# Linear attention and a feed-forward pair on one core: where the loads of batch 1 are issued, and three smaller edits

## The chip, the cores and the metric

The kernel runs on one NeuronCore of a Trainium2 chip, as one program. The metric is the device time of one execution in microseconds (us). The core has a matrix engine (TensorE, here PE), a vector engine (VectorE, DVE), a scalar engine (ScalarE, ACT), a general engine (GpSimd, POOL or Pool) and an engine that issues DMAs (SyncE, SP). ACT and Pool issue DMAs too. Each engine runs its own instructions in order; 16 DMA engines move the data. SBUF is the memory on the core, PSUM the accumulators of PE.

## The reference

Inputs are q, k and v of shape (8, 8, 576, 64), that is batch, heads, sequence, head width, and two weight matrices of 512 x 2048 and 2048 x 512, all float32. The output is 4608 x 512 in float32.

```python
theta = np.pi / 2.0 * pos / S
cos_w, sin_w = np.cos(theta), np.sin(theta)      # along the sequence
def phi(x, c, s):
    r = np.maximum(x, 0.0)
    return np.concatenate([r * c, r * s], axis=-1)
q_p, k_p = phi(q, cos_w, sin_w), phi(k, cos_w, sin_w)
kv = np.einsum('bhsf,bhsd->bhfd', k_p, v)
z = np.sum(k_p, axis=2)
num = np.einsum('bhsf,bhfd->bhsd', q_p, kv)
den = np.einsum('bhsf,bhf->bhs', q_p, z)[..., None] + 1e-06
attn = num / den
x = attn.transpose(0, 2, 1, 3).reshape(B * S, H * D)
h = x @ w_in
g = h * (1.0 / (1.0 + np.exp(-1.702 * h)))
out = g @ w_out
```

## The kernel before

The attention of batch b gives columns of xT, a bf16 tensor of 128 partitions x 4 x 4608 tokens in SBUF. The feed-forward pair runs over nine blocks of 512 tokens. Block i takes 32 steps: 16 of mm1 (four matmuls of 128 x 512, then the activation by ACT) and 16 of mm2 (four matmuls each; every fourth step ends one chunk t of 128 tokens, which is copied to ysb and stored). The attention of batch b = i + 1 is cut into pieces, and a list `work[n]` puts each piece behind step n of block i. The schedule is written out by hand: each engine gets its instructions in the order of the program. Batch 0 runs ahead of the loop, and warm-up matmuls on zeros fill PE there (L75).

For each batch, q, k and v come as three main loads (`load_mains`, rows 0 to 511 of the sequence, 1 MB each, runs of 1 KB) and three tail loads (`load_tails`, rows 512 to 575, 128 KB each, runs of 256 bytes). SP issues both in batches 1 to 7; in batch 0 ACT issues the tails. q goes through max(x, 0) into qn (L217), is transposed by PE for batches 0 and 1 (L240) and by DMA later (L251), and is multiplied by cos and sin into qT (L244 or L256). v is multiplied by cos and sin into vt (L277), k goes through max into kr. `unit_kv` (L288) forms kv and z, `unit_den` the denominator (L309, L313) and its reciprocal (L318), `unit_spread` (L333) spreads that over partitions, `unit_num` (L351) forms the numerator, and L354 writes xT.

The weights are loaded by Pool in four quarters each. DMAs and copies of one element into `junk` are put in the queues as gates: SP's first one (L432) waits for the third quarter of w_in and stands ahead of the loads of batch 1; Pool's (L436) waits for batch 1's v and stands ahead of w_out; SP's second one (L439) waits for the third quarter of w_out and stands ahead of the loads of batch 2. Loads of batch 3 and later are issued at step 1 of the block two before.

In `unit_den` a matmul with three rows of constants (L309) puts 1e-6 into the accumulator, and the 32 matmuls of L313 add to it. The copies of mm2 go to ysb, which has three buffers, so the fourth chunk reuses the first's; in block 0 chunks 1 and 3 are copied by DVE (L401), all others by ACT (L403). SP issues all stores (L405). A chunk of 128 tokens is stored in one or two pieces; the last of all has two.

Of the kernel before, what the change touches and what calls it, by code (L numbers as in the profile page):

```python
# [12 lines left out]
F32 = mybir.dt.float32  # L13
# [8 lines left out]
ADD = mybir.AluOpType.add  # L22
# [6 lines left out]
def kernel(  # L29
# [9 lines left out]
    nc = tc.nc  # L39
    B, H, S, D = q.shape  # L40
    d_model = H * D
    d_ff = moe_w_in.shape[1]
    NP = H // 2
    FC = d_ff // 128
    TB = 512
    NBLK = B * S // TB
    HF = S // 2
    NSEG = 4
    SEG = S // NSEG
# [13 lines left out]
    def hps_tile():  # L63
        return ps.tile([128, TB], F32, name="hps", bufs=2)

    def yps_tile():
        return ps.tile([128, TB], F32, name="yps", bufs=2)

    def at_tile():
        return ps.tile([128, TB], F32, name="at", bufs=4)  # L70

    def warmup(n):
        for _ in range(n):
            wps = hps_tile()
            nc.tensor.matmul(wps, warm[:, 0:128], warm, start=True, stop=True)  # L75
# [8 lines left out]
    def load_tail(t, src, b, on):  # L84
        on.dma_start(
            out=t[0:64, 2048:2560].rearrange("p (h d) -> p h d", h=H),
            in_=src[b, :, 512:576, :].rearrange("h p d -> p h d"))
# [7 lines left out]
    def load_tails(b, on):  # L95
        for name, src in SRC:
            load_tail(state[b][name], src, b, on)
# [64 lines left out]
    ypool = ctx.enter_context(tc.tile_pool(name="ypool", bufs=3))  # L162
# [17 lines left out]
    ones = const.tile([3, 128], BF16)  # L180
    epsm = const.tile([3, SEG], BF16)
# [19 lines left out]
    w_in_sb = one.tile([128, NP, d_ff], BF16)  # L201
    w_out_sb = one.tile([128, FC, d_model], BF16)
# [16 lines left out]
    def prep_q(b, par, on=nc.vector):  # L219

        s = state[b]
        o = s["qn"].rearrange("p c (jo par hh) d -> p par c jo hh d", par=2, hh=2)[:, par]
        i = s["qf"][:, 0:2048].rearrange("p (jo par hh c d) -> p par c jo hh d", par=2, hh=2, c=4, d=D)[:, par]
        it = s["qf"][0:64, 2048:2560].rearrange("p (jo par hh d) -> p par jo hh d", par=2, hh=2, d=D)[:, par]
        for n in range(2):
            if par == 0:
                relu(on, o[:, 0:4, n], i[:, :, n])
            else:
                relu(on, o[:, 0:4, :, 1 - n], i[:, :, :, n])
                relu(on, o[0:64, 4, :, 1 - n], it[:, :, n])  # L230
        if par == 0:
            relu(on, o[0:64, 4], it)

    def transpose_pe(b, j, step):
        s = state[b]
        if step == 0:
            s["tp", j] = tp = at_tile().bitcast(BF16)
            for c in range(5):
                np_ = 128 if c < 4 else 64
                nc.tensor.transpose(tp[:, c * 128:c * 128 + np_],  # L240
                                    s["qn"][:np_, c, 2 * j:2 * j + 2, :].rearrange("p h d -> p (h d)"),
                                    ident[:np_, :np_])
            return
        nc.vector.tensor_tensor(s["qT"][:, j], s["tp", j][:, 0:S].unsqueeze(1).to_broadcast([128, 2, S]), trig, op=MUL)  # L244
# [13 lines left out]
    def prep_k(b, h0, h1, on=nc.vector):  # L258
        relu(on, kr[:, 0:4, h0 // 2:h1 // 2].rearrange("p c j (hh d) -> p (j hh) c d", hh=2),
             state[b]["kf"][:, 256 * h0:256 * h1].rearrange("p (h c d) -> p h c d", c=4, d=D))  # L260
# [44 lines left out]
    def unit_den(b):  # L305

        s = state[b]
        den_ps = at_tile()
        nc.tensor.matmul(den_ps[:, 0:SEG], ones[0:3, :], epsm[0:3, :], start=True, stop=False)  # L309
        for g in range(NSEG):  # L310
            for cs in range(2):
                for j in range(NP):
                    nc.tensor.matmul(den_ps[32 * j:32 * j + 32, 0:SEG], s["zs"][:, j, cs, ds(12 - 4 * g, 32)],  # L313
                                     s["qT"][:, j, cs, ds(g * SEG, SEG)],
                                     start=False, stop=(g == NSEG - 1 and cs == 1))
        inv, pa, pb, comb = [two.tile([128, SEG], dt, name=f"den{n}", bufs=1)
                             for n, dt in enumerate((F32, F32, F32, BF16))]
        nc.vector.reciprocal(inv, den_ps[:, 0:SEG])  # L318
        for o, m in ((pa, 0), (pb, 1)):
            nc.vector.tensor_tensor(o.bitcast(I32), inv.bitcast(I32), bits[:, m:m + 1].to_broadcast([128, SEG]), op=AND)  # L320
        nc.vector.tensor_tensor(comb, pa, pb, op=SUB)
        s["comb"] = comb
        s["invb"] = {}
# [33 lines left out]
    gT = {}  # L357
# [16 lines left out]
    def pieces(m):  # L374

        got, g = [], m * 128
        while g < m * 128 + 128:
            b, r = divmod(g, S)
            if r < 512:
                n = min(128 - r % 128, m * 128 + 128 - g)  # L380
                got.append((g - m * 128, n, b * S + 4 * (r % 128) + r // 128, 4))
            else:
                n = min(S - r, m * 128 + 128 - g)
                got.append((g - m * 128, n, b * S + r, 1))
            g += n
        return got
# [3 lines left out]
    def mm2(i, t, part):  # L390

        if part == 0:
            cur[t] = hps_tile() if i == 0 and t < 2 else yps_tile()
        yps = cur[t]
        for fc in range(part * 4, part * 4 + 4):
            nc.tensor.matmul(yps, gT[fc][:, ds(t * 128, 128)], w_out_sb[:, fc, :],  # L396
                             start=(fc == 0), stop=(fc == FC - 1))
        if part == 3:
            ysb = ypool.tile([128, d_model], F32, name="ysb")
            if i == 0 and t % 2:  # L400
                nc.vector.tensor_copy(ysb, yps)  # L401
            else:
                nc.scalar.copy(ysb, yps)  # L403
            for (p0, n, row, step) in pieces(i * 4 + t):
                nc.sync.dma_start(out=out[row:row + (n - 1) * step + 1:step, :], in_=ysb[p0:p0 + n, :])  # L405


    junk = const.tile([1, 16], F32)
    AC, PO = nc.scalar, nc.gpsimd
    prep_new(0)  # L410
    prep_q(0, 0)
    prep_q(0, 1, AC)
    warmup(26)
    for j in range(NP):
        transpose_pe(0, j, 0)
    for j in range(2):
        transpose_pe(0, j, 1)
    for c in range(5):
        prep_v(0, c, 0)
# [3 lines left out]
    prep_k_tail(0)  # L423
    prep_k(0, 0, 4, AC)
    prep_k(0, 4, 8)
    for j in range(2, NP):
        transpose_pe(0, j, 1)

    nc.gpsimd.tensor_copy(junk[:, 0:1], s0["vf"][0:1, 0:1])
    for g in range(4):  # L430
        nc.gpsimd.dma_start(out=w_in_sb[:, :, ts(g, 512)], in_=win_r[:, :, ts(g, 512)])  # L431
    nc.sync.dma_start(out=junk[:, 8:9], in_=w_in_sb[0:1, 0, 1534:1536].bitcast(F32))  # L432
    load_new(1)
    load_mains(1)
    load_tails(1, nc.sync)
    nc.gpsimd.tensor_copy(junk[:, 1:2], state[1]["vf"][0:1, 0:1])  # L436
    for g in range(4):
        nc.gpsimd.dma_start(out=w_out_sb[:, ts(g, 4), :], in_=wout_r[:, ts(g, 4), :])
# [3 lines left out]
    unit_kv(0)  # L442
    warmup(4)
    unit_den(0)
    warmup(8)
    for hf in range(2):
# [12 lines left out]
    for i in range(NBLK):  # L459
        work = {n: [] for n in range(40)}  # L460
        b = i + 1

        def at(n, f, *a):
            work[n].append(lambda: f(*a))

        if b < B:
            k0 = 6 if i == 0 else 0
            at(k0, prep_new, b)
            at(k0, prep_q, b, 0)
            at(k0, prep_q, b, 1)  # L470
            if i == 0:
                for j in range(NP):
                    at(k0 + 2 + j, transpose_pe, b, j, 0)
                    at(k0 + 2 + j, transpose_pe, b, j, 1)
            else:
                at(k0, transpose_dma, b)
                if b + 1 < B:
                    at(k0 + 1, load_all, b + 1)
            for c in range(5):
                for cs in range(2):  # L480
                    at(k0 + 2 + c, prep_v, b, c, cs)
            at(k0 + 7, prep_k, b, 0, 4)
            at(k0 + 7, prep_k_tail, b)
            at(k0 + 8, prep_k, b, 4, 8)
            if i > 0:
                for j in range(NP):
                    at(k0 + 9 + j, prep_trig, b, j)
            k1 = 15 if i == 0 else 12
            at(k1, unit_kv, b)
            at(k1 + 3, unit_den, b)  # L490
            for hf in range(2):
                at(k1 + 7 + 6 * hf, unit_spread, b, hf)
                at(k1 + 10 + 6 * hf, unit_num, b, hf)
        for n in range(32):
            if n < FC:
                if i > 0 or n > 3:
                    mm1(i, n)
            elif i == 0:
                mm2(i, n % 4, (n - FC) // 4)
            else:  # L500
                mm2(i, (n - FC) // 4, n % 4)
            for f in work[n]:
                f()
        for n in range(32, 40):
            for f in work[n]:
                f()
# [30 lines left out]
```

## Time and profile before

| | us |
|---|---|
| median of 8 runs | 323.53 |
| lowest and highest | 322.9 and 324.34 |
| profiled execution, its own time | 324.34 |
| span of the profiled execution | 322.1 |

| engine | busy us | share of the span | instructions |
|---|---|---|---|
| PE matmul | 303.3 | 94% | 2173 |
| PE weight load | 140.1 | 43% | 2212 |
| DVE | 132.4 | 41% | 336 |
| ACT | 135.7 | 42% | 260 |
| POOL | 16.2 | 5% | 52 |

The span runs from the first to the last instruction, 2.2 us less than the time of the same execution. A line such as "L360 PE" names line 360 of the kernel; "x16" counts instructions. PE's busy time is modelled and overlaps its weight loads, so it is read together with its waits. PEclk is the share of PE's full clock that was granted. In the list of waits each line says who waited, for whom, for how long in total, how often, and the longest. In the chain of waits each line has a start, a duration and what went on. In the timeline a line has a start, a duration, the instruction, and in brackets the idle time before it.

### The profile page before, as it was taken

What the parts mean: (1) busy time and instruction counts of PE and PEld (TensorE: products, weight loads), DVE (VectorE), ACT (ScalarE), POOL (GpSimd) and SP (SyncE); (2) the same over time, 40 slices, a digit from 0 to 9 for tenths busy, and PEclk for the clock granted to TensorE, in tenths of its full rate; (3) what the DMA queues carried; (4) which work ended last, traced back from release to release, by engine and by line L of the source; (5) the groups of instructions that cost most, each with busy time, mean ns of one, the idle gap of its engine ahead of it and who ended that gap; (6) DMA issues with size and microseconds to landing.
All of it is one profiled execution on the core that took longest, in us unless ns stands there. A gap on an engine that the chain in (4) does not pass through costs nothing.

```text
span 322.1 us, 5478 instructions
## 1 busy us (share of the span) xinstructions
PE 303.3 (94%) x2173; PEld 140.1 (43%) x2212; DVE 132.4 (41%) x336; ACT 135.7 (42%) x260; POOL 16.2 (5%) x52
## 2 busy tenths in 40 slices
PE   8999099989999999999999999999999999999993
PEld 3444045434544454445444544454444444444441
DVE  4761096267616471755174617461754110000000
ACT  5545022146333734372436243624372447217511
POOL 7800300000000000000000000000000000000000
PEclk9999879999999999999999999999999999999999
DMA  7999997934972598259626972594330220011022
GB/s 219 261 206 275 235 201 242 206 135 85 350 136 67 87 330 175 81 89 354 124 67 93 348 141 82 125 342 99 77 64 0 68 65 2 33 65 33 2 65 65
DMA packets 62188, 45.83 MB, mean 142 GB/s; under 512 B 28884, under 2 KB 57556, under 8 KB 62164
## 3 DMA queue, kind: packets, MB, share of 16 engines
q1 hardware_dynamic: 56356, 40.90, 49.1%
q0 software_dynamic: 4224, 4.19, 8.3%
q10 hardware_dynamic: 1584, 0.39, 0.6%
q8 instruction: 17, 0.28, 0.4%
q14 instruction: 7, 0.06, 0.1%
HBM read 36.70 MB, written 9.44 MB: 143 GB/s over the span
## 4 chain that ended last, share of the span: by engine, by line
PE 85%; DMA 10%; SPq 1%; issue 1%; POOL 1%; DVE 0%; ACT 0%; DVEq 0%; ACTq 0%
PE yps L396 37%; PE hps L360 37%; DMA qf<-in_q_dram 4%; DMA vf<-in_v_dram 3%; DMA w_in_sb<-in_moe_w_in_dram 3%; PE at L288 3%; PE at L351 3%; PE hps L396 2%; PE at L313 1%; PE at L333 1%; SPq L80 1%; POOL w_in_sb L431 1%; PE at L240 0%; PE at L309 0%; SPq L432 0%
## 5 line engine op out<-in xcount | busy, mean ns | idle before, releaser
L360 PE MATMUL hps<-xT,w_in_sb 128*128 128x512 bf16 x551 | 127.5, 382 | 2.0 <-DVE xT L354 0.9
L396 PE MATMUL yps<-w_out_sb,g 128*128 128x512 bf16 x524 | 122.7, 380 | 1.2 <-issue 0.2
L365 ACT ACTIVATE g<-hps 128x512 bf16<-128x512 f32 x142 | 84.7, 597 | 63.6 <-PE hps L360 61.9
L360 PEld LDWEIGHTS <-w_in_sb 128*128 128x128 bf16 x576 | 55.6, 98 | 69.2 <-issue 5.0
L396 PEld LDWEIGHTS <-g 128*128 128x128 bf16 x576 | 53.5, 98 | 65.2 <-issue 2.9
L403 ACT COPY ysb<-yps 128x512 f32<-128x512 f32 x33 | 19.3, 586 | 87.2 <-PE yps L396 65.1
L354 DVE TENSOR_TENSOR xT<-at,invb 128x288 bf16<-128x288 f32 x64 | 24.7, 450 | 64.4 <-PE at L351 64.4
L338 ACT COPY invb<-at 128x288 f32<-128x288 f32 x60 | 19.7, 420 | 18.7 <-PE at L333 18.7
L256 DVE TENSOR_TENSOR qT<-qTr,trig 128x1152 bf16<-128x1152 bf16 x24 | 16.6, 754 | 22.9 <-DMA qTr<-qn 22.9
L217 DVE TENSOR_SCALAR qn<-qf 128x512 bf16<-128x512 f32 (+2 forms) x52 | 14.3, 341 | 16.8 <-DMA qf<-in_q_dram 16.8
L277 DVE TENSOR_SCALAR vt<-vf,cosw 128x512 bf16<-128x512 f32 (+1 forms) x40 | 18.9, 481 | 0.1
L277 DVE TENSOR_SCALAR vt<-vf,sinw 128x512 bf16<-128x512 f32 (+1 forms) x36 | 17.0, 473 | 0.0
L75 PE MATMUL hps<-warm 128*128 128x512 bf16 x52 | 14.7, 442 | 1.2 <-DVE halfpi L121 1.2
L318 DVE RECIPROCAL den<-at 128x144 f32<-128x144 f32 x8 | 8.5, 1058 | 13.5 <-PE at L313 13.5
L351 PE MATMUL at<-qT,kvs 64*64 64x288 bf16 x256 | 12.2, 289 | 0.4 <-ACT invb L338 0.3
L217 DVE TENSOR_SCALAR kr<-kf 128x1024 bf16<-128x1024 f32 (+1 forms) x23 | 12.5, 596 | 0.0
L240 PE MATMUL at<-ident,qn 128*128 128x128 bf16 (+1 forms) x40 | 4.4, 227 | 8.0 <-DVE qn L217 8.0
L288 PE MATMUL at<-vt,kr 128*64 128x130 bf16 x320 | 10.6, 221 | 0.7 <-ACT kr L215 0.7
L288 PEld LDWEIGHTS <-kr 128*64 128x64 bf16 x320 | 9.3, 109 | 4.2 <-issue 2.5
L351 PEld LDWEIGHTS <-kvs 64*64 64x64 bf16 x256 | 6.4, 105 | 8.0 <-issue 7.7
L75 PEld LDWEIGHTS <-warm 128*128 128x128 bf16 x52 | 5.4, 110 | 8.8 <-issue 3.6
L240 PEld LDWEIGHTS <-qn 128*128 128x128 bf16 (+1 forms) x40 | 3.2, 102 | 10.7 <-DVE qn L217 8.2
(69 smaller groups left out, 88.4 us busy)
## 6 DMA issues: line engine op xcount, KB each, us to landing
qf<-in_q_dram SPq DMA_DIRECT2D x8, 1024.0 KB, 6.3
vf<-in_v_dram SPq DMA_DIRECT2D x8, 1024.0 KB, 9.1
kf<-in_k_dram SPq DMA_DIRECT2D x7, 1024.0 KB, 12.7
out_dram<-ysb SPq DMA_DIRECT2D x40, 128.0 KB, 2.3
out_dram<-ysb SPq DMA_DIRECT2D x16, 256.0 KB, 2.3
w_in_sb<-in_moe_w_in_dram POOLq DMA_DIRECT2D x4, 512.0 KB, 8.7
w_out_sb<-in_moe_w_out_dram POOLq DMA_DIRECT2D x4, 512.0 KB, 11.7
kf<-in_k_dram SPq DMA_DIRECT2D x2, 512.0 KB, 11.3
```

The costliest lines, as they stand in the source:

```text
L75: nc.tensor.matmul(wps, warm[:, 0:128], warm, start=True, stop=True)
L217: on.tensor_scalar(o, i, 0.0, None, op0=MAX)
L256: nc.vector.tensor_tensor(s["qT"][:, j], s["qTr"][:, j].unsqueeze(1).to_broadcast([128, 2, S]), trig, op=MUL)
L277: on.tensor_scalar(o, i, w, None, op0=MUL)
L288: nc.tensor.matmul(kv4[j // 2][w:w + 64, j % 2], kr[:, c, j, 64 * hh:64 * hh + 64], vt[:, c, 2 * j + hh, :], start=(c == 0), stop=(c == 4))
L338: nc.scalar.copy(invb, bps[j][:, 0:HF])
L351: nc.tensor.matmul(num_ps[j][w:w + 64, 0:HF], s["kvs"][j][r:r + 64, cs, :], s["qT"][r:r + 64, j, cs, ds(hf * HF, HF)], start=(cs == 0), st ...
L354: nc.vector.tensor_tensor(xT[:, j, ds(b * S + hf * HF, HF)], t[:, 0:HF], s["invb"][j, hf], op=MUL)
L360: nc.tensor.matmul(hps, w_in_sb[:, kc, ds(fc * 128, 128)], xT[:, kc, ds(i * TB, TB)], start=(kc == 0), stop=(kc == NP - 1))
L365: nc.scalar.activation(g, hps, AF.Gelu_apprx_sigmoid)
L396: nc.tensor.matmul(yps, gT[fc][:, ds(t * 128, 128)], w_out_sb[:, fc, :], start=(fc == 0), stop=(fc == FC - 1))
L403: nc.scalar.copy(ysb, yps)
```

## The change

Batch 1's mains are issued once the second quarter of w_in has landed, instead of the third. Batch 1's tails leave SP's queue for Pool's, where they stand behind w_in and a new copy that waits for its third quarter. In batch 0 all four qT products stand ahead of v on DVE, and 21 warm-up matmuls precede the transposes instead of 26. In batches 1 to 7 L309 goes, and DVE adds 1e-6 into `pa` before the reciprocal. The last chunk of the last block is computed in two halves of 256 columns, the first copied by ACT, the second by DVE, and the two pieces of each are stored from SP and from ACT.

```diff
@@ unit_den
         den_ps = at_tile()
-        nc.tensor.matmul(den_ps[:, 0:SEG], ones[0:3, :], epsm[0:3, :], start=True, stop=False)
+        if b == 0:
+            nc.tensor.matmul(den_ps[:, 0:SEG], ones[0:3, :], epsm[0:3, :], start=True, stop=False)
...
-                                     start=False, stop=(g == NSEG - 1 and cs == 1))
+                                     start=(b > 0 and g == 0 and cs == 0), stop=(g == NSEG - 1 and cs == 1))
...
-        nc.vector.reciprocal(inv, den_ps[:, 0:SEG])
+        if b == 0:
+            nc.vector.reciprocal(inv, den_ps[:, 0:SEG])
+        else:
+            nc.vector.tensor_scalar(pa, den_ps[:, 0:SEG], 1e-6, None, op0=ADD)
+            nc.vector.reciprocal(inv, pa)
@@ new function
+    def mm2_last(i, t):
+        yps = yps_tile()
+        ysb = ypool.tile([128, d_model], F32, name="ysb")
+        hd = d_model // 2
+        for n in range(2):
+            cols = ds(n * hd, hd)
+            if n == 1:
+                yps = yps_tile()
+            for fc in range(FC):
+                nc.tensor.matmul(yps[:, 0:hd], gT[fc][:, ds(t * 128, 128)], w_out_sb[:, fc, cols],
+                                 start=(fc == 0), stop=(fc == FC - 1))
+            if n == 0:
+                nc.scalar.copy(ysb[:, cols], yps[:, 0:hd])
+            else:
+                nc.vector.tensor_copy(ysb[:, cols], yps[:, 0:hd])
+            for m, (p0, cnt, row, step) in enumerate(pieces(i * 4 + t)):
+                (nc.sync if m == 0 else nc.scalar).dma_start(out=out[row:row + (cnt - 1) * step + 1:step, cols],
+                                                             in_=ysb[p0:p0 + cnt, cols])
@@ batch 0
-    warmup(26)
+    warmup(21)
     for j in range(NP):
         transpose_pe(0, j, 0)
-    for j in range(2):
+    for j in range(NP):
         transpose_pe(0, j, 1)
...
-    for j in range(2, NP):
-        transpose_pe(0, j, 1)
...
-    nc.sync.dma_start(out=junk[:, 8:9], in_=w_in_sb[0:1, 0, 1534:1536].bitcast(F32))
+    nc.sync.dma_start(out=junk[:, 8:9], in_=w_in_sb[0:1, 0, 1022:1024].bitcast(F32))
     load_new(1)
     load_mains(1)
-    load_tails(1, nc.sync)
+    nc.gpsimd.tensor_copy(junk[:, 2:3], w_in_sb[0:1, 0, 1534:1535])
+    load_tails(1, nc.gpsimd)
     nc.gpsimd.tensor_copy(junk[:, 1:2], state[1]["vf"][0:1, 0:1])
...
@@ the loop over blocks
+            elif i == NBLK - 1 and n >= 28:
+                if n == 28:
+                    mm2_last(i, 3)
             else:
                 mm2(i, (n - FC) // 4, n % 4)
```

## The prediction

> **What bounds the kernel now.** I read the 40 slices first, then the list of waits, the chain of waits, the timeline of 60 to 70 us, and last the DMA packets in one-microsecond windows.
>
> The slices say that TensorE (PE) is full but for one slice near 34 us. The waits and the chain name what it waited for there:
>
> ```profile
> PE   8999099989999999999999999999999999999993
> ...
> PE at L240 <- DVE qn L217: 8.0, 1, 8.0
> DVE qn L217 <- DMA qf<-in_q_dram: 16.8, 3, 9.0
> ...
> 27.39 12.85 DMA qf<-in_q_dram
> ```
>
> PE stands still from 32.6 to 40.6 us: the transposes of batch 1 (L240) need the tail rows of q. Their DMA was issued at 27.39 behind the 3 MB of batch 1's q, v and k on SP's queue and landed at 40.2. The clock then makes it worse. In these windows the columns after the window are its length, busy PE, weight load, DVE, ACT and POOL, then PEclk, DMA share, GB/s:
>
> ```profile
> 24.00:25.00 1.00, 0.97 (x4) 0.43 (x6) 0.97 (x3) 0.00 (x0) 0.00 (x0) 1.00 0.90 146
> 25.00:26.00 1.00, 0.98 (x5) 0.49 (x5) 0.00 (x0) 0.00 (x0) 0.00 (x0) 1.00 0.38 56
> ...
> 36.00:37.00 1.00, 0.00 (x0) 0.00 (x0) 0.00 (x0) 0.00 (x0) 1.00 (x3) 1.00 1.36 129
> 37.00:38.00 1.00, 0.00 (x0) 0.00 (x0) 0.00 (x0) 0.00 (x0) 0.49 (x1) 0.76 1.49 155
> 38.00:39.00 1.00, 0.00 (x0) 0.00 (x0) 0.00 (x0) 0.00 (x0) 0.00 (x0) 0.50 1.51 161
> ...
> 43.00:44.00 1.00, 1.00 (x4) 0.39 (x4) 0.72 (x2) 0.29 (x1) 0.00 (x0) 0.50 1.24 205
> 44.00:45.00 1.00, 1.00 (x8) 0.54 (x6) 0.83 (x3) 0.19 (x1) 0.00 (x0) 0.82 1.25 209
> ```
>
> PEclk falls to 0.50 at about 37.3, 4.7 us into the idle time, and is back at about 44.2. From 40.6 to L288 at 49.94 PE takes 9.3 us for some 7.4 us of work at full clock: 1.9 us lost. Also to be seen: the DMA engines are full from 14 to 48 us but for a hole of some 2 us at 25, and the 256-byte tail packets alone (36 to 37) move only 129 GB/s.
>
> The second place to read is where batch 1 meets block 1:
>
> ```profile
> 65.23 3.79 SPq L405 DMA_DIRECT2D out_dram<-ysb  x4
> ...
> 67.97 0.69 DVE L401 COPY ysb<-yps 128x512 f32<-128x512 f32 x1 [1.45 <-PE at L351]
> ...
> 68.58 1.54 DVE L354 TENSOR_TENSOR xT<-at,invb 128x288 bf16<-128x288 f32 x4
> 69.08 3.20 PE L360 MATMUL hps<-xT,w_in_sb 128*128 128x512 bf16 x11 [0.94 <-DVE xT L354]
> ```
>
> ysb has three buffers, so the fourth output copy of block 0 (67.97) reuses the first and must wait until the first store has landed. That store was issued at 65.23 and lands 2.4 to 2.6 us later, about 67.75. Behind this copy on DVE stand the last xT products (L354) and behind those all of PE's block 1. And SP, which issues the store, first has to issue the six loads of batch 2. Those start at the landing of the third quarter of w_out (48.59); their last packet is moved at 64.9. So in the kernel before, this DMA chain is within some 2 us of PE. That decides the forecast.
>
> **Part 1: mains at the second quarter of w_in, tails on Pool.** The quarters of w_in land at 17.8, 20.3, 23.8 and 26.4 (issue plus time to landing). SP issues three mains some 3.5 us earlier, at 21.1 instead of 24.6, and no tails (6.9 us of issues that stood only ahead of its wait for w_out). Pool adds one 1x1 copy (0.18), which waits for the third quarter at about 24, and three tail DMAs at 0.75 to 1.1 us each (w_out's and w_in's issues). Behind them on Pool is only the copy that gates w_out, which waits for v's main anyway (34.4): the issues end at 27.5 and are covered. From Pool's issue to flowing packets took 2.8 us for w_out (34.5 to 37.3) and 2.9 for w_in, so q's tail flows from 27. Batch 0, whose tails are on ACT's queue, shows such a mixture: 239 main and 239 tail packets in the same microsecond (7 to 8), one for one. At that rate 512 tail packets take 2.15 us, and with 1 to 1.7 us to the semaphore q's tail lands at 30.3 to 31.2. PE wants it at 32.4: the stall and its slow clock go. Next late is DVE: from 33.0 four qT products of 0.67 and ten v products of 0.395 take it to 39.7, the first k product to 40.4; L288 starts at about 40.7 instead of 49.94. PE would be 9.2 us ahead.
>
> **But the DMA chain is not.** With 1:1 sharing v's main lands at about 33.5 (34.34 before), w_out is issued at 33.7, flows from 36.5 free of tails at 205 packets/us, and its third quarter lands at 36.8 + 7.5 + 1.7 to 2.9 us of laggard engines: 46.0 to 47.2, say 46.6 (48.59 before). Batch 2's loads are unchanged: last packet 16.3 us after that gate (48.59 to 64.9), so 62.9. The first store, ready at 56, lies behind them in the same queue; with about 0.8 us of rows and 0.6 to the semaphore it lands at 64.3. DVE's copy follows, and PE starts 1.1 us after it (67.97 to 69.08): 65.5 instead of 69.08. Gain 3.6 us, not 9.2. PE has idled since 59, over 6 us.
>
> Two rules of the Trainium skill bear on this. *Row:* 129 GB/s for tails alone, some 300 in batch 0's mixture, and a hole at 25. *Rule:* "DMA: Bandwidth & Descriptors", section Issuing engines are not separate DMA queues: all issuing engines share 16 DMA engines and interleave, so a second queue saves issue time only. By the rule the gate stays at 48.59, PE starts at 67.5, and 1.6 us are won, which would make the sum below 322.4; by the rows it is 3.6 us and 320.4. I take the rows, since mixing and filling the hole are this case's own numbers, and keep the rule for the upper end. *Row:* the clock fell 4.7 us into idleness and came back 3.6 us after work resumed; at the start of the kernel warm-up matmuls ran slow for some 5.8 us. *Rule:* "TensorE: Matmul & The Clock Gate", section Part 1: the windows are free-running, about 3.4 us, so the fall comes anywhere from 3.4 us on. An idle time of 6 us very likely falls. Half of 3.6 to 5.8 us is 1.8 to 2.9 lost; I take 2.1. Without the fall it is 0.
>
> **Part 2: q's trig products ahead of v in batch 0.** Five warm-up matmuls of 0.216 fewer let the transposes start at 8.65 instead of 9.57 (q's first half is ready at 8.1). Four products of 0.7 on DVE then end at 12.1, so v begins 0.4 later than 11.70, but two products no longer stand behind k: zbuf's copies come 0.4 to 0.6 earlier. Den still waits for the four warm-up matmuls that end at 17.55. Bounds: 0.4 either way; taken 0, hidden by those matmuls and by k on ACT (15.27).
>
> **Part 3: eps.** PE loses L309 in batches 1 to 7: 0.17 us in the chain each, of which a bubble may stay (144 columns at full clock are 0.06). DVE gains one PSUM read of 128x144, 0.2 to 0.3 (the row of L320 is 0.305), ahead of the reciprocal. Den's chain on DVE ends 1.5 us before L333 needs it (87.90 against 89.38), so it is covered. Batch 1's share drowns in the store's wait; six times 0.15 is 0.9.
>
> **Part 4: halves at the end.** 32 matmuls of 256 columns at about 0.109 for 16 at 0.216: +0.04, as the transposes' pitch of 0.07 with a full weight load each says that loading does not bind. Copying half a tile on DVE is 0.42 (L302's row) for 0.58; the second store no longer follows the first on SP (1.11 for two issues); half the bytes remain (1.3 us of data). Together about 0.75, bounds 0.2 and 1.2.
>
> **Sum.** 3.6 - 2.1 + 0.9 + 0.75 = 3.15 us. The profiled execution took 324.34 (span 322.1), the slowest of eight and 0.8 above the median, 323.53. From the median: 320.4.
>
> **Rivals.**
> - *The store's wait is small.* Stores pass the tails, or these no longer lag. For it: most engines finish tails 14.6 us after the gate, not 16.3. Against: one queue, in order. With the gate at 46 and no clock fall PE starts at 63, and the gain is 6.1 + 1.65, about 315.8; with no wait at all 9.2 + 1.1 + 0.75, 312.5.
> - *Slower.* Mains share engines with w_in's rest and then with the tails, so v's main lands later, w_out with it, and the store. Gate plus 18.9 is PE's start; with the clock's 2.1 the whole is a loss from a gate of 49.7 on (69.08 + 1.65 - 2.1 - 18.9), that is if v's main lands after about 36.6, where I put it at 33.5 and it was 34.34. A microsecond beyond that gives 324.5. Against it: the mains start 3.5 us earlier, and w_in's rest is some 300 packets.
> - *The change doesn't do what it says:* tails on Pool land after 36. PE then idles earlier and less later, and the store's wait hides it: 320 to 322.
>
> **How the numbers follow.** Store's wait as summed, gate between 46 and 48.6, clock loss 0 to 2.9: chance 0.75, by itself 318 to 322.5. Small or no wait: 0.15. Slower or level through a late gate: 0.1, half of it beyond. The range takes the first case whole and reaches into both others: 316.8 to 323.1. A measurement of this kernel can tell about 0.2% (0.65 us) from no change: faster 0.85, same 0.07, slower 0.08.
>
> **What would show it.** Right: no wait at L240; L288 of batch 1 near 41; w_out's third quarter landing at 46 to 47; a new wait of 5 to 7 us at block 1's first matmul behind DVE's xT, with DVE's ysb copy idle until the first store has landed at about 64; PEclk at 0.50 for 3 to 6 us after that. Wrong: the first store landing before 60, or an unchanged stall at L240.

## The result and the profile after

| | before | after |
|---|---|---|
| median, us | 323.80 (32 runs) | 319.12 (11 runs) |
| lowest and highest | 322.69 and 325.37 | 317.3 and 320.47 |
| profiled execution, its time and span | 324.34, 322.1 | 320.39, 318.4 |

The ratio is 0.9859, with a 95% interval from 0.984 to 0.9877: 4.7 us faster, where the prediction's sum was 3.15 us and its time 320.4. The profiled execution of after is, like that of before, one of the longer ones, 1.3 us above the median.

First the slices of after, PE's busy tenths and its granted clock (each slice is 8 us):

```profile
PE   8699969669999999999999999999999999999994
PEclk9999999979999999999999999999999999999999
```

The empty slice of before, 32 to 40 us, is gone. The next one (40 to 48) is partly empty now, and so are the two from 56 to 72 us; the clock's dip has moved to the ninth slice. The list of waits names the new wait:

```profile
DVE ysb L406 <- DMA out_dram<-ysb: 5.3, 1, 5.3
PE hps L365 <- DVE xT L359: 4.8, 1, 4.8
...
PE at L288 <- DVE kr L217: 2.4, 1, 2.4
```

L406 is L401 of before, L365 is L360 and L359 is L354. PE lost 8.0 us at L240 before; now it loses 2.4 us at batch 1's L288 and 4.8 us at the first matmul of block 1. The timeline (start, duration, what, and in brackets the idle time before it) shows both. First batch 1's loads and who takes them:

```profile
21.70 0.76 SPq L455 DMA_DIRECT2D junk<-w_in_sb  x1
...
23.82 0.71 POOL L85 DMA_DIRECT2D qf<-in_q_dram  x1
...
31.48 1.23 DVE L217 TENSOR_SCALAR qn<-qf 64x256 bf16<-64x256 f32 x5 [0.92 <-DMA qf<-in_q_dram]
...
35.69 0.49 DVE L277 TENSOR_SCALAR vt<-vf,cosw 128x512 bf16<-128x512 f32 x1 [2.11 <-DMA vf<-in_v_dram]
...
42.76 1.70 PE L288 MATMUL at<-vt,kr 128*64 128x130 bf16 x40 [2.44 <-DVE kr L217]
...
48.55 0.60 SPq L463 DMA_DIRECT2D junk<-w_out_sb  x1
```

q's tail, issued by Pool at 23.82, lands at 31.4 and PE does L240 at 32.26 without a pause. v's main lands at 35.66, 1.3 us later than before, and DVE is late with k: L288 starts at 42.76 (49.94 before). The last row is the gate, the landing of w_out's third quarter: 48.55 against 48.59. It hasn't moved at all. The two rows of before:

```profile
48.59 0.64 SPq L439 DMA_DIRECT2D junk<-w_out_sb  x1
...
49.94 1.36 PE L288 MATMUL at<-vt,kr 128*64 128x130 bf16 x40
```

Then the boundary of block 1, after:

```profile
59.55 6.34 SPq L410 DMA_DIRECT2D out_dram<-ysb  x4
...
64.84 0.69 DVE L406 COPY ysb<-yps 128x512 f32<-128x512 f32 x1 [5.34 <-DMA out_dram<-ysb]
65.45 1.54 DVE L359 TENSOR_TENSOR xT<-at,invb 128x288 bf16<-128x288 f32 x4
65.95 5.17 PE L365 MATMUL hps<-xT,w_in_sb 128*128 128x512 bf16 x15 [4.84 <-DVE xT L359]
```

The first store is issued at 59.55 and takes 5.17 us. The fourth copy, xT and PE follow it. In before the same store held PE back by some 0.4 us (e11 below); now PE has been idle for 4.84 us. The windows (length, busy PE, weight load, DVE, ACT, POOL, PEclk, DMA share, GB/s) give the clock:

```profile
65.00:66.00 1.00, 0.05 (x1) 0.05 (x1) 1.00 (x3) 0.00 (x0) 0.00 (x0) 0.86 0.04 16
66.00:67.00 1.00, 1.00 (x3) 0.35 (x3) 1.00 (x4) 0.00 (x0) 0.00 (x0) 0.50 0.61 233
...
68.00:69.00 1.00, 1.00 (x3) 0.40 (x3) 1.00 (x5) 0.45 (x1) 0.00 (x0) 0.50 0.00 0
69.00:70.00 1.00, 0.86 (x5) 0.43 (x5) 1.00 (x4) 0.57 (x1) 0.00 (x0) 0.93 0.01 2
```

A mean of 0.86 in the first row puts the clock's fall at about 65.7, one of 0.93 in the last its return at 69.1; three matmuls per us in the rows between, where four or more are normal, are its price.

The two traces add up so, in us of lead over before:

| milestone | before | after | lead |
|---|---|---|---|
| L288 of batch 1 | 49.94 | 42.76 | 7.18 |
| first matmul of block 1 | 69.08 | 65.95 | 3.13 |
| L288 of batch 2 | 81.04 | 79.03 | 2.01 |
| L288 of batch 3 | 113.08 | 110.90 | 2.18 |
| end of PE | 317.17 | 314.21 | 2.96 |
| end of the span | 322.1 | 318.4 | 3.7 |

So 7.2 us are won at batch 1, 4.1 of them are given back to the store and 1.1 more to the clock; eps and the end add 1.7. The times of these two executions differ by 3.95 us, so 0.25 us are won outside the span.

### The profile page after: what moved, and what is told of

It is laid out like the page before. It is cut to its first block, busy times and chain, and to the rows that moved or that the text cites. A ratio compares the mean times of both kernels' runs of the same rounds, so it can differ in the third digit from the quotient of the medians.

```text
span 318.4 us, 5510 instructions
## 1 busy us (share of the span) xinstructions
PE 299.6 (94%) x2178; PEld 140.0 (44%) x2216; DVE 135.6 (43%) x344; ACT 135.5 (43%) x260; POOL 18.5 (6%) x56
## 3 DMA queue, kind: packets, MB, share of 16 engines
q1 hardware_dynamic: 54772, 40.38, 47.6%
## 4 chain that ended last, share of the span: by engine, by line
PE 82%; DMA 12%; DVE 3%; issue 1%; SPq 1%; POOL 0%; DVEq 0%
PE yps L401 36%; PE hps L365 35%; DMA vf<-in_v_dram 7%; DMA w_in_sb<-in_moe_w_in_dram 3%; PE at L288 3%; PE at L356 3%; PE hps L401 2%; DMA out_dram<-ysb 2%; DVE vt L277 1%; PE at L314 1%; PE yps L422 1%; PE at L338 1%; DVE qT L244 1%; DVE kr L217 0%; POOL w_in_sb L454 0%
## 5 line engine op out<-in xcount | busy, mean ns | idle before, releaser
L365 PE MATMUL hps<-xT,w_in_sb 128*128 128x512 bf16 x551 | 127.1, 382 | 6.0 <-DVE xT L359 4.8
L401 PE MATMUL yps<-w_out_sb,g 128*128 128x512 bf16 x509 | 118.8, 380 | 0.9 <-issue 0.2
L370 ACT ACTIVATE g<-hps 128x512 bf16<-128x512 f32 x142 | 84.7, 597 | 58.9 <-PE hps L365 56.2
L365 PEld LDWEIGHTS <-w_in_sb 128*128 128x128 bf16 x576 | 55.7, 98 | 73.2 <-issue 9.1
L401 PEld LDWEIGHTS <-g 128*128 128x128 bf16 x560 | 51.9, 98 | 63.4 <-issue 2.9
L359 DVE TENSOR_TENSOR xT<-at,invb 128x288 bf16<-128x288 f32 x64 | 24.7, 450 | 62.0 <-PE at L356 62.0
L277 DVE TENSOR_SCALAR vt<-vf,cosw 128x512 bf16<-128x512 f32 (+1 forms) x40 | 18.9, 481 | 2.3 <-DMA vf<-in_v_dram 2.3
L277 DVE TENSOR_SCALAR vt<-vf,sinw 128x512 bf16<-128x512 f32 (+1 forms) x36 | 17.4, 484 | 0.0
L288 PE MATMUL at<-vt,kr 128*64 128x130 bf16 x320 | 10.9, 221 | 4.5 <-DVE kr L217 2.4
L75 PE MATMUL hps<-warm 128*128 128x512 bf16 x47 | 12.4, 417 | 1.2 <-DVE halfpi L121 1.2
L288 PEld LDWEIGHTS <-kr 128*64 128x64 bf16 x320 | 9.3, 109 | 8.2 <-DVE kr L217 3.2
L75 PEld LDWEIGHTS <-warm 128*128 128x128 bf16 x47 | 4.6, 105 | 7.2 <-issue 1.9
L401 PE MATMUL hps<-w_out_sb,g 128*128 128x512 bf16 x30 | 7.6, 380 | 0.1
L323 DVE RECIPROCAL den<-den 128x144 f32<-128x144 f32 x7 | 7.4, 1053 | 0.2
```

The source lines that it names most:

```text
L277: on.tensor_scalar(o, i, w, None, op0=MUL)
L288: nc.tensor.matmul(kv4[j // 2][w:w + 64, j % 2], kr[:, c, j, 64 * hh:64 * hh + 64], vt[:, c, 2 * j + hh, :], start=(c == 0), stop=(c == 4))
L359: nc.vector.tensor_tensor(xT[:, j, ds(b * S + hf * HF, HF)], t[:, 0:HF], s["invb"][j, hf], op=MUL)
L365: nc.tensor.matmul(hps, w_in_sb[:, kc, ds(fc * 128, 128)], xT[:, kc, ds(i * TB, TB)], start=(kc == 0), stop=(kc == NP - 1))
L370: nc.scalar.activation(g, hps, AF.Gelu_apprx_sigmoid)
```

## The experiments

Each kernel is the changed one with one more edit, unless it says otherwise. The ratios are to before, run on the same chip. The theory: two separate gains, loads and small edits, the first of them cut short by the wait for the first store. The rivals: the store's wait costs little; the gate or the clock decides; Pool's queue is without influence.

### The parts apart: e3_no_load_part, and e5_after_again

Before's gate, mains and tails, with all the rest of the change:

```diff
-    nc.sync.dma_start(out=junk[:, 8:9], in_=w_in_sb[0:1, 0, 1022:1024].bitcast(F32))
+    nc.sync.dma_start(out=junk[:, 8:9], in_=w_in_sb[0:1, 0, 1534:1536].bitcast(F32))
...
-    nc.gpsimd.tensor_copy(junk[:, 2:3], w_in_sb[0:1, 0, 1534:1535])
-    load_tails(1, nc.gpsimd)
+    load_tails(1, nc.sync)
```

> The changed kernel with batch 1's loads as they were before (mains behind the third quarter of w_in, tails from SP); the eps, the order in batch 0 and the halves at the end stay. Theory: seven matmuls L310 at 0.16 us and 0.75 us at the end, batch 0 nothing: about 321.9 us, so that the loads are worth some 2.8 us of the 4.7. Rival (the loads brought nothing, the small edits everything): 319.1. Rival (the loads brought all): 323.8.

Measured: 321.66 us (19 runs), 0.9933 [0.9916, 0.995]. Before was 323.95 there, so the small edits bring 2.3 us; from 321.66 to after's 319.12 the loads bring some 2.5. Nearly 0.4 us of these lie outside the span: by medians an execution takes 2.33 us more than its span in e3 and 1.96 in after.

The changed kernel itself once more, beside e6 to e8:

> The changed kernel once more, unchanged, as the base for the runs beside it on the same chip: 319.1 us, between 317.3 and 320.5 in single executions.

Measured: 319.45 us (6 runs), 0.987 [0.9844, 0.9896]. Its trace is not the same as the first. v's main was 1 us later, L288 of batch 1 started at 43.78 after an idle time of 2.82 us, and there the clock fell, from 44.5 to 47.9:

```profile
44.00:45.00 1.00, 0.95 (x26) 0.68 (x22) 0.86 (x4) 0.00 (x0) 0.00 (x0) 0.75 1.22 202
45.00:46.00 1.00, 1.00 (x21) 0.83 (x18) 0.14 (x1) 0.00 (x0) 0.00 (x0) 0.50 1.26 209
```

So PE came to the end of block 0 2.5 us later and waited for the store 2.24 us only. The gate is at 48.83, block 1 starts at 65.86 as in the first trace, the clock stays at 1.00 there, and L288 of batch 2 stands at 77.83 instead of 79.03. A fall ahead of the store's wait is hidden by it; a fall behind it costs a microsecond. None of the executions of after and e5 on record has a mean granted clock above 0.995, while the traces without a fall while PE works (e1, e9, e10) have 0.997 or more: very likely the clock fell somewhere in each.

### The store's wait: e1_ysb4, e9_one_more_ysb, e11_before_one_more_ysb

e1 gives ysb a fourth buffer, so that the fourth copy of block 0 needn't wait for the first store:

```diff
-    ypool = ctx.enter_context(tc.tile_pool(name="ypool", bufs=3))
+    ypool = ctx.enter_context(tc.tile_pool(name="ypool", bufs=4))
```

> The changed kernel with four ysb buffers in place of three, so that the fourth output copy of block 0 no longer reuses the first one's buffer. Theory (block 1 waits for the first store, which is queued behind batch 2's loads): the wait of 5.3 us before L406 goes, block 1's first matmul comes about 1.1 us after the last numerator (61.1), at about 62.2 instead of 65.95, and PEclk no longer falls there (another 1.1 to 1.6 us): about 314.3 us against 319.1. Rival A (another limit stands close behind, such as batch 2's q tail or its transposes): a wait moves to L288 or L314 of batch 2 and the gain is 1 to 2 us. Rival B (the store has nothing to do with it, PE waits for xT's own chain): no change.

Measured: 315.96 us (5 runs), 0.976 [0.9726, 0.9793]. The fourth copy runs at 60.63 after PE, block 1 starts at 61.74, the clock stays at 1.00, and L288 of batch 2 is at 73.70, 5.3 us earlier. But the median gains 3.2 us only. The rest is lost evenly later: the period from one batch's L288 to the next is 32.09 us where it was 31.87. PE's weight loads tell of it; here the wait rows of e1 and of after (total, times, longest):

```profile
PEld L365 <- issue: 10.3, 56, 0.5
```

```profile
PEld L365 <- issue: 9.1, 19, 4.8
```

After has 19 such waits, one of them the 4.8 us at block 1; e1 has 56 small ones. In e1's program, 14 of the 16 activations L370 of each later block wait for an earlier instruction of ACT itself beside the wait for PE; in the changed kernel only those of block 1 do. In the trace the second wait is an instruction of its own, 113 times at this line in e1 and 15 times in after and in e9:

```profile
L370 ACTq EVENT_SEMAPHORE  x113: 17/17/38, 27.3 to 296.8; - x113
```

e9 tests this reading: ysb keeps its three buffers and the waits of after, and a single extra tile takes the fourth chunk.

```diff
-            ysb = ypool.tile([128, d_model], F32, name="ysb")
+            ysb = (ysx if i == 0 and t == 3 else ypool.tile([128, d_model], F32, name="ysb"))
...
+    ysx = const.tile([128, d_model], F32, name="ysx")
```

> The changed kernel, with one more tile ysx of 128x512 that only chunk 3 of block 0 uses; ysb keeps three buffers, so the waits of the later blocks' activations stay as in the changed kernel. Theory (the wait for the first store costs 4.8 us and its clock fall, and what e1_ysb4 gave back in the later blocks came from the additional waits of its activations): L288 of batch 2 at 73.7 as in e1_ysb4 (79.0 in the changed kernel), the period of a batch 31.84 again and not 32.08, PE's end near 309.2, time 314.2 to 314.6. Rival (the longer period belongs to any kernel whose block 1 isn't held back, or to the larger SBUF use): period 32.08, time 316.0.

Measured: 315.19 us (6 runs, 313.89 to 317.18), 0.9749 [0.9718, 0.9779]. In its trace (an execution of 314.1 us) block 1 starts at 60.87, and no copy waits for a store:

```profile
59.76 0.69 DVE L406 COPY ysx<-yps 128x512 f32<-128x512 f32 x1 [1.03 <-PE yps L401]
...
60.87 2.12 PE L365 MATMUL hps<-xT,w_in_sb 128*128 128x512 bf16 x7 [0.53 <-DVE xT L359]
```

L288 of batches 2 and 3 stand at 72.84 and 104.71: a period of 31.87 again. The wait row of the weight loads is

```profile
PEld L365 <- issue: 3.5, 14, 0.5
```

so e1's loss in the later blocks belongs to the additional waits, not to a freed block 1. The medians of e1 and e9 don't separate them: three of e9's six executions took 316.0 to 317.2 us. These have mean granted clocks of 0.994, 0.994 and 0.987, where the trace has 0.997, so the clock probably fell in them. At 0.997 or more e1's four executions took 315.8 to 316.7 us and e9's two 313.9 and 314.1. But one of e9 at 0.992 took 314.4, and no trace shows where the falls were; what each of them cost stays open.

The same extra tile in the kernel before:

> The kernel before with the extra tile of e9 alone. Theory (there the store's wait is hidden by the stall at L240 and holds PE for 0.94 us at most, so the buffer is only worth something together with the change): L288 of batch 1 stays at 49.9, L288 of batch 2 at 80.1 to 81.0, time 322.6 to 323.3. Rival (the buffer alone brings what it brought the changed kernel): 319 to 320.

Measured: 323.48 us (14 runs), 0.9993 [0.9976, 1.001]. L288 of batch 1 stays at 49.79; PE's wait at block 1 goes from 0.94 to 0.53. The buffer is worth nothing before and 4 us after: it is the change that brings PE up against the store.

### The gate: e12_third_quarter_gate, e2_tails_act, e7_tails_act_again

e12 returns one line, the mains behind w_in's third quarter, and leaves the tails on Pool:

```diff
-    nc.sync.dma_start(out=junk[:, 8:9], in_=w_in_sb[0:1, 0, 1022:1024].bitcast(F32))
+    nc.sync.dma_start(out=junk[:, 8:9], in_=w_in_sb[0:1, 0, 1534:1536].bitcast(F32))
```

> The changed kernel with batch 1's mains behind the third quarter of w_in again; tails stay on Pool. Theory (the DMA engines are the bound up to the first store, so what they idle at 25 us comes back as a later third quarter of w_out): a hole of 1 to 2 us in the transfers at 25, v's main at 36.5 to 37.5, the third quarter of w_out at 49.5 to 50.5, block 1's start at 67 to 68, time 320.2 to 321.2. Rival (the mains only share with w_in and the tails, so their start is worth nothing): the third quarter of w_out within 0.5 of 48.5, time within 0.5 of the changed kernel's 319.1 to 319.5.

Measured: 319.89 us (6 runs), 0.9879 [0.9855, 0.9904], the rival. The mains are issued at 24.68 instead of 22.51, yet v's main lands at 35.96 instead of 35.66, L288 of batch 1 is at 43.05, the gate at 47.97. There is no stall at L240 either. The earlier mains earn nothing that these runs can tell; what ended the stall is that the tails no longer stand behind the mains.

In e2 and e7, one kernel run at two times, ACT issues the tails after batch 0's invb copies, with no gate of their own:

```diff
-    nc.gpsimd.tensor_copy(junk[:, 2:3], w_in_sb[0:1, 0, 1534:1535])
-    load_tails(1, nc.gpsimd)
...
+    load_tails(1, nc.scalar)
```

> The changed kernel with batch 1's tails issued from ACT's queue ahead of its first activations instead of from Pool. Theory (Pool's tail packets are large, 0.1 MB in some 35 packets per microsecond, and take turns with 1 KB packets of the mains, so v's main came 2 us late): ACT's packets are of 256 bytes, mains keep some 240 KB per microsecond, v's main lands at 34 to 34.7 instead of 35.66, w_out's third quarter at 47.3 to 47.8 instead of 48.55, and block 1 starts about 1 us earlier: 318 us. Rival (all queues share the engines, only the sum of bytes counts): w_out's third quarter at 48.5 again, no change in time.

> The kernel with batch 1's tails on ACT's queue again, beside the changed kernel on one chip. Its trace had w_out's third quarter at 46.3 and block 1 at 63.4. Theory: that is 2 to 2.5 us ahead of the changed kernel and shows in the medians as 1.5 to 2 us less. Rival (the traces fell at two ends of the spread and the queue of the tails makes no difference): medians within 0.5 us.

Measured: 318.84 us (6 runs), 0.9856 [0.9817, 0.9895], and 319.27 us (6 runs), 0.9876 [0.9851, 0.9902]: no difference from after in the medians. The traces do differ: v's main lands at 34.4 and 34.0, the gate is at 46.34 and 46.22, block 1 starts at 63.43 and 63.00, 2.5 and 2.9 us earlier. The clock takes back a part: from there to L288 of batch 2 it takes 13.54 and 14.24 us (13.08 in after, 11.96 without a fall). Beside e5, whose clock had fallen ahead of the store's wait, e7's lead shrinks from 2.9 to 0.6 us that way. Another part is lost outside the span: an execution takes 2.42 us (e2) and 2.44 (e7) more than its span, by medians, for 1.96 in after and 1.95 in e5. What these 0.5 us are isn't shown.

Why the gate moves can be read from the DMA queues (packets, MB, share of the 16 engines' time) in 3 us of mixed transfers. After, 28 to 31 us, q1 being SP's queue and q0 Pool's:

```profile
q1 hardware_dynamic: 407, 0.41, 62.1%
q0 software_dynamic: 106, 0.31, 47.4%
```

e2, 27 to 30 us, q10 being ACT's:

```profile
q1 hardware_dynamic: 784, 0.79, 86.5%
q10 hardware_dynamic: 655, 0.16, 26.3%
```

From ACT the tails are packets of 256 bytes and take turns with the mains' 1 KB almost one for one, at 317 GB/s together. From Pool they are packets of 2.9 KB, each of which holds an engine for some 0.2 us (47.4% of 16 engines' 3 us, over 106 packets; 0.05 for a packet of the mains in e2). The mains get half as many packets through, and both together move 244 GB/s. k's tail lands at 34.2 (35.6 in e2), but v's main later, and w_out's issue hangs on v's main. That the queue's kind does it, and not the tails' start some 1 to 3 us earlier in e2 and e7, was not separated.

### The store's queue: e6_stores_act, e8_tails_and_stores_act

Block 0's stores leave SP, where batch 2's loads are ahead of them, for ACT; e8 does so on top of e2's edit:

```diff
-                nc.sync.dma_start(out=out[row:row + (n - 1) * step + 1:step, :], in_=ysb[p0:p0 + n, :])
+                (nc.scalar if i == 0 else nc.sync).dma_start(
+                    out=out[row:row + (n - 1) * step + 1:step, :], in_=ysb[p0:p0 + n, :])
```

> The changed kernel with block 0's four stores issued from ACT's queue instead of SP's; three ysb buffers as before, the fourth copy still waits for the first store. Theory (the store waits because it stands behind batch 2's loads in one queue): the first store is issued at 58.2 and takes turns with the loads' packets, lands at 60.5 to 61.5 instead of 64.7, block 1 starts at 62 to 62.6, PEclk does not fall: 4.5 to 5 us less, about 314.3. Rival (the DMA engines are full, and a store gets through only once the loads are done, whatever its queue): landing at 63 to 64.7, gain below 1 us.

> Both moves to ACT's queue: batch 1's tails and block 0's stores. Theory: with the store's wait gone PE alone sets the time, and what remains of the tails' move is only that L288 of batch 1 comes somewhat earlier (42.30 for 42.76 with the tails on ACT alone): 313.8 to 314.3, at best 0.5 us below the stores' move alone. Rival (gains add): 2 us below it.

Measured: 318.69 us (6 runs), 0.9851 [0.9815, 0.9886], and 318.58 us (6 runs), 0.985 [0.982, 0.988]: no difference from after (319.45 in e5) nor from e7. e6's trace says little of the queue: the clock fell at batch 1 there (45.4 to 48.9), and the store was issued at 60.96, later than SP's in after. e8's rows:

```profile
57.57 0.36 ACTq L410 DMA_DIRECT2D out_dram<-ysb  x1
...
61.95 0.69 DVE L406 COPY ysb<-yps 128x512 f32<-128x512 f32 x1 [3.10 <-DMA out_dram<-ysb]
63.06 3.02 PE L365 MATMUL hps<-xT,w_in_sb 128*128 128x512 bf16 x7 [2.60 <-DVE xT L359]
```

The first store still takes 4.3 us. In e2, where SP issued it at 57.76 behind batch 2's loads, it took 4.4, and block 1 started at 63.43. What it passes through is to be seen in one of e8's windows:

```profile
58.00:59.00 1.00, 1.00 (x6) 0.45 (x5) 0.69 (x1) 0.97 (x4) 0.00 (x0) 1.00 1.37 147
```

The engines are full (share above 1) and slow (147 GB/s), with batch 2's 256-byte tails among the store's rows. In after, e2 and e5 to e8 the first store is issued between 56.53 and 60.96, and the copy that waits for it runs 15.7 to 16.5 us after the gate, whatever the queue. So the wait is for the engines, which batch 2's loads keep full (in after the DMA share is 1.05 and more from 52 to 64 us), rather than for a place in the queue; how the engines share their time between the two queues was not taken further.

### The clock: e4_fill

22 warm-up matmuls ahead of block 1's first matmul:

```diff
+                if i == 1 and n == 0:
+                    warmup(22)
```

> The changed kernel with 22 warm-up matmuls on zeros (4.75 us at full clock) put ahead of block 1's first matmul, so that PE works through the idle time of 4.84 us. They add no result. Theory (the idle time costs a second time through the clock): PEclk stays at 1.00 and the time falls by 1.1 to 1.6 us, to about 317.7. Rival (block 1's first matmuls are paced by xT anyway, or the warm-up runs over its time): within 0.3 us of 319.1.

Measured: 319.2 us (6 runs), 0.9858 [0.9823, 0.9893]. The clock stays at 1.00 there, and from block 1's start to L288 of batch 2 it takes 11.52 us instead of 13.08. But in this trace (320.57 us) the clock had fallen at batch 1, from 44.2 to 47.6 as in e5, so PE came to the end of block 0 at 62.9 instead of 61.1. The warm-ups end at 67.6, some 2 us after xT would have let PE start (the fourth copy ran at 64.47, and PE follows it by 1.1), and block 1 starts at 67.59: the two cancel. The three executions at a mean clock of 0.997 or more, so without such a fall, took 318.25 to 318.69 us, the three at 0.993 took 319.71 to 320.57. So the fill may gain half a microsecond where it isn't late; that, and fewer warm-ups, was not taken further. The clock's cost in after is 1.1 us (against 11.96 in before and e1) to 1.6 us (against 11.52).

### Both together: e10_one_more_ysb_tails_act

With e9's tile in place block 1 no longer waits for the gate and the store, so batch 1's L288 should count.

> As e9_one_more_ysb, with batch 1's tails issued by ACT as in e2_tails_act. Theory (with the store out of the way, only L288 of batch 1 counts, which stood 0.5 and 1.7 us earlier with ACT's tails, 42.30 and 41.07 for 42.76): 0.3 to 1.7 us under e9, 313 to 314. Rival (block 1's start is set by PE's and DVE's own work after the end of batch 1): the same time as e9 within 0.3. Other rival: ACT's issues delay batch 0's copies, and it is slower than e9 by up to 1.

Measured: 313.56 us (4 runs, 313.1 to 313.87), 0.9688 [0.9671, 0.9705]: the fastest of all, 10.1 us under before and clear of e9's interval. L288 of batches 1 and 2 stand at 41.42 and 72.28, each 0.56 before e9's trace. The medians differ by more, 1.6 us, since e9's median takes in its three longer executions.

## Why the prediction was right, and where it wasn't

**The bound of the forecast.** "The DMA chain is not [ahead]": this was the step that mattered, and it holds. PE reached batch 1's L288 7.2 us earlier, and all but 3.1 us of it was gone at block 1. e1, e9 and e11 show that the first store is what took it.

**The stall at L240.** Predicted to go, q's tail at 30.3 to 31.2: it began to flow at 28.0 instead of 27 and landed at 31.4. L288 was put at 40.7 and came at 42.76. The term that was off is v's main: predicted at 33.5, it landed at 35.66, DVE waited 2.1 us for it at L277 and ended k that much later. The mains' issue was also later than summed, 22.51 for 21.1, since w_in's second quarter landed at 21.67 and not at 20.3 as in the trace of before. e12, with still later mains, shows no cost of this last error.

**The gate.** Here the weighing of rule and row failed. *Row:* the gate stands at 48.55, 48.59 before. *Rule:* the Trainium skill's "DMA: Bandwidth & Descriptors", section Issuing engines are not separate DMA queues, says that DMAs run on the same 16 engines whoever issues them, and would have left it at 48.59; the prediction took the rates of batch 0's mixture instead and put it at 46.6. That mixture was ACT's queue with SP's, and e2, e7, e8 and e10 reach 46.1 to 46.3 with it, which the rule taken alone doesn't give. Pool's is another: 244 GB/s for 317, and a gate of 46.88 to 48.83 in the seven traces with its tails (after, e1, e4, e5, e6, e9, e12). The hole at 25 us did fill, from 56 to 331 GB/s, and was paid back later, as the windows of after show:

```profile
30.00:31.00 1.00, 1.00 (x7) 0.42 (x5) 0.56 (x2) 0.50 (x2) 0.00 (x0) 1.00 1.08 181
31.00:32.00 1.00, 1.00 (x6) 0.45 (x5) 0.52 (x2) 0.73 (x2) 0.00 (x0) 1.00 1.09 196
```

In before, with the mains alone, these two microseconds moved 355 and 346 GB/s.

**From the gate to the store.** 17.7 us were summed (46.6 to 64.3), 16.2 measured (48.55 to 64.72). Too early a gate and too long a way cancelled; that the start of block 1 came out at 65.95 for 65.5 is luck. "In the same queue" was given as the reason for the store's wait; e8 beside e2 shows that another queue doesn't shorten it.

**The clock.** A loss of 2.1 us was taken from "half of 3.6 to 5.8 us"; it was 1.1 in this trace. The low clock of before, from which the 3.6 was read, lasted 6.8 us (37.5 to 44.4 by the windows, where the prediction read 37.3 and 44.2); here it lasted 3.4. It came back at 69.1, 3.2 us after work resumed, and half of that is 1.6, which is what e4 gives. The difference to 1.1 is PE's waiting for the later parts of xT, which it does at full clock too (11.96 us in e1) and not in e4 (11.52), where xT was complete.

**The small edits.** Batch 0's order: 0 predicted; the first matmul of mm1 is at 23.97, 23.93 before. Eps: 0.15 per batch predicted, 0.16 measured in the period (31.84 for 32.00 over the later batches). The end: PE's end to the span's end is 4.18 for 4.92, a gain of 0.74 for 0.75. Together 1.65 predicted, 1.7 in the traces, and 2.3 in e3's median; what the rest there is isn't shown.

**The sum.** Loads 3.6 - 2.1 = 1.5 us predicted, 3.1 - 1.1 = 2.0 in the traces, some 2.5 in the medians: this is the term that was too small. In the traces the gain was half a microsecond smaller than summed and the clock's loss a whole one. Of what the medians have beyond that, 0.25 to 0.4 us lie outside the span, of which the sum knew nothing; and an execution whose clock falls ahead of the store's wait, as e5's, loses less behind it.

## What to carry to other kernels

When a stall is removed, look at the next buffer that the faster engine will find occupied, and follow it back to the transfer that frees it: here one tile of 256 KB was worth 3.9 us on top of the change's 4.7, and nothing without it. Before adding a buffer to a pool in the steady loop, see whether the rotation adds waits elsewhere; an extra tile for the one instance that needs it left the loop alone. A rate read from one pair of queues need not hold for another. And look for the clock in the whole trace, not only where a fall is expected: what e4 and e5 mean came out only with their falls at batch 1.

## What the runs showed of the hardware

- *The clock can fall sooner than the prediction had it, and even after the wait has ended.* It allowed a fall "anywhere from 3.4 us on". Taking a window's mean clock as one step from 1.00 to 0.50, the fall at block 1 came 2.1 us after block 0's last matmul in e6, 2.4 in e7, 3.4 in e8, 4.3 in e12 and 4.6 in after; in e8 and e12 PE had resumed by then. At batch 1 it came 1.3, 0.7 and 1.6 us after PE had resumed from 2.57, 2.82 and 3.12 us of idle time (e4, e5, e6). At block 1 an idle time of 2.25 us ended in a fall in e6, one of 2.24 in e5 didn't:

```profile
65.00:66.00 1.00, 0.00 (x0) 0.00 (x0) 1.00 (x3) 0.00 (x0) 0.00 (x0) 0.96 0.16 57
66.00:67.00 1.00, 0.90 (x3) 0.35 (x3) 1.00 (x4) 0.00 (x0) 0.00 (x0) 0.50 0.44 170
```

```profile
66.00:67.00 1.00, 1.00 (x4) 0.23 (x3) 1.00 (x4) 0.00 (x0) 0.00 (x0) 1.00 0.67 256
```

  (First e6, then e5.)
- *A longer wait isn't a dearer one.* Summed over the windows, each fall while PE had work lasted 3.4 us (after, e2, e4, e5, e6, e8, e12) or 6.8 us (before, e3, e7, e11), and no other time was seen. After 4.84 us of idle time it was 3.4 in after, after 3.57 us it was 6.8 in e7. From block 1's start to L288 of batch 2 it then took 12.89 us in e6, 13.08 in after and 14.24 in e7.
- *A wait for one's own engine has a price.* In e1 every second activation starts 0.03 to 0.06 us later after PE than in e9 (an idle time of 0.30 to 0.33 for 0.27); from one batch to the next this came to 0.22 us for PE (32.09 for 31.87).
- *The same 256-byte runs travel differently by issuer:* as 256-byte packets from ACT, as packets of some 2.9 KB from Pool (0.16 MB in 655 packets, 0.31 MB in 106).
